# Gathers of a routed expert layer issued in pairs behind the matmul steps, and tile places reused oldest first

## The chip, the cores and the metric

The kernel runs on one core of a Trainium2 chip. The metric is the device time of one execution in microseconds (us). The engines are TensorE (PE, with its weight loads PEld), VectorE (DVE), ScalarE (ACT), GpSimd (POOL) and SyncE (SP, which issues most transfers). Each engine works its own instructions in the order of its own stream, and engines wait for each other by semaphores. An indirect gather is issued by POOL, which is busy while it does so; the rows land some microseconds later.

## The reference

Three layers follow each other on 2304 tokens of 512 numbers (4 x 8 heads x 576 x 64), all in 32-bit floats:

```python
kv = np.einsum('bhsd,bhse->bhde', k, v)                 # linear attention
out = np.einsum('bhsd,bhde->bhse', q, kv)
x = out / rms(out) * g_norm                             # 2304 x 512

top2 = np.argpartition(-noisy_logits, 2, axis=1)[:, :2] # 8 experts, 2 per token
for e in range(E):
    for k in range(2):
        mask = top2[:, k] == e
        h = np.maximum(x[mask] @ w1[e], 0.0)            # 512 -> 1024
        out[mask] += top2_w[mask, k, None] * (h @ w2[e])  # 1024 -> 512

gate = 1.0 / (1.0 + np.exp(-(x @ w_gate)))              # second layer, 512 -> 1536
return (gate * (x @ w_val)) @ w_out                     # 1536 -> 512
```

## The kernel before

**Numbers.** A 32-bit float goes through PE as two parts: ACT writes the high part (a tile whose name ends in h), DVE the rest (it ends in l), and a product takes three matmuls: high by high, high by low, low by high.

**Stages.** Up to about 130 us come the attention, the routing and expert e0. Experts e1 to e7 follow until about 549 us. Then comes the second layer: its first steps (up to about 575), its products (two chunks of the tokens, six pieces of the width, seven products per piece, which are added and subtracted to give a 2 x 2 block product), and from about 820 us the steps of the output.

**An expert.** Each expert takes up to 624 rows, in five blocks of 128. It has eight *h steps* (`h_step`, line 756 within `h_half`): 24 matmuls of 312 columns into `ph`, of which PSUM holds two. ACT then writes `hh` (line 761) and DVE `hl` (line 762); both must be done before PE's step after next, which writes the same `ph`. Five *y steps* follow (`y_step`, line 800): 24 matmuls of 512 columns into `py`, which ACT copies to `yo` and SP stores in `ybuf`.

**Gathers.** The rows of expert e+1 are gathered while e runs. `gather` (lines 687 to 697, through `rows_of`) issues four indirect gathers of quarter rows per block into an `xg` tile; there are four such tiles, so a gather waits until DVE has transposed the block that held its tile (line 743). `scale` (line 716) multiplies a block by its routing weights, on POOL. In the y phase `expert_in` takes a block in: DVE's transpose (743), ACT's `xh` (746), DVE's `xl` (747). In the loop over h steps, `gather(e + 1, i)` stands in steps 0 to 3 and `scale(e + 1, i - 1)` in steps 1 to 4, all in POOL's program order; the fifth block is gathered and scaled in the y phase. Nothing ties POOL to PE's steps: it runs as far ahead as its tiles allow. Beside this DVE sums and splits weights (lines 604 to 637, `raw`, `wg`, `wv`, `w_..`), paced by a planner (`pump`).

**The second layer's gathers.** `fetch` issues two gathers (`yg`, from `ybuf`) per tile of 128 tokens, which ACT scales and DVE adds. Tiles 0 to 3 are fetched within e7. Those of tiles 4 to 9, twelve gathers, stand one behind another in front of the layer's first steps. The first steps' matmuls are `pgv` (line 1121), the transposes `px` (1019); ACT copies the result to `q` (1129) and DVE multiplies it.

**Places.** The tiles of the second layer stand in places: 28 of the pool `wp` (`free`) and 11 of `g4` (`extra`). `place` takes the next of `free` while there is one, else one of `extra`; `drop` and `put_back` give places back. A tile that takes a place waits for whatever still reads the tile before it: a matmul, or a store of it. In the output steps `gr` is loaded from `qbuf`, and `gh_..h` (ACT, line 976) and `gh_..l` (DVE, line 977) are split from it for the matmuls `poa`, `pob`, `poc` (line 1332). The stores of `qt`, `qv` and `q` are lines 1197 to 1199.

**Order.** POOL and SP run in program order, DVE too after e0, PE and ACT in the second layer; in the experts a scheduler orders PE and ACT.

Of the kernel before, what the change touches and what calls it, by code (L numbers as in the profile page):

```python
# [9 lines left out]
FT = mybir.dt.float32  # L10
# [62 lines left out]
def tile_linear_attention_moe_glu(  # L73
# [16 lines left out]
    nc = tc.nc  # L90
# [11 lines left out]
    NB = CAP_BLOCKS  # L102
# [9 lines left out]
    QW = DM // 4 + KD  # L112
# [6 lines left out]
    WHOLE = CHUNKS[0][1]  # L119
# [4 lines left out]
    sml = ctx.enter_context(tc.tile_pool(name="sml", bufs=2))  # L124
# [14 lines left out]
    free = deque(range(28))  # L139

    def take(shape, dt, name):

        i = free.popleft()
        return i, wp.tile(shape, dt, tag="w", name=name)

    def wt(shape, dt, name):

        i, t = take(shape, dt, name)
        free.append(i)
        return t  # L150
# [7 lines left out]
    def et(shape, dt, name):  # L158
        return ep.tile(shape, dt, tag="e", name=name)
# [33 lines left out]
    first = ctx.enter_context(ExitStack())  # L193
# [16 lines left out]
    for i in range(B // 2):  # L210
        x = wt([128, 2, H, D], FT, f"vrem{i}")
# [35 lines left out]
    x, y = KD * 2 * E, KD * 2 * E + NT * E  # L247
# [327 lines left out]
    raws, wst, places, whole = deque(), {}, {}, set()  # L575
# [81 lines left out]
        return True  # L657

    def put_back(u):
        free.extend(places.pop(u))  # L660

    def pump(work_of_pe, own=0.0):

# [13 lines left out]

    XG, XA, XL, HH, HL = {}, {}, {}, {}, {}

    def whole_rows(e, blk):  # L680

        return e == 0 or e == 1 and blk < 2

    def gather(e, blk):
        if whole_rows(e, blk):
            x = et([128, XW], FT, "xg")
            a = e == 0 and blk < AB
            ix = lsa[:, blk:blk + 1] if a else lsb[:, blk * E + e:blk * E + e + 1]
            rows_of(x, xbuf[0:NA, :] if a else xbuf, ix)
        else:  # L690
            x = et([128, 4, QW], FT, "xg")
            for b in range(4):
                rows_of(x[:, b], xbuf.rearrange("n (a w) -> (n a) w", a=4), lsq[:, b, blk * E + e:blk * E + e + 1])
        XG[e, blk] = x

    def rows_of(x, src, ix):
        nc.gpsimd.indirect_dma_start(out=x, out_offset=None, in_=src,  # L697
                                     in_offset=bass.IndirectOffsetOnAxis(ap=ix, axis=0))
# [9 lines left out]
    def scale(e, blk, eng):  # L708
        x = XG[e, blk]
        if whole_rows(e, blk):  # L710
            i, t = take([128, DM], FT, f"xs{e}_{blk}")
            XG[e, blk] = scaled_rows(x, eng, t)
            places["xs", e, blk] = i,
        else:
            xv = x[:, :, 0:128].rearrange("p b (c j) -> p b c j", j=32)
            eng.tensor_mul(xv, xv, x[:, :, 128:, None].to_broadcast([128, 4, KD, 32]))  # L716
# [214 lines left out]
    def fetch(t):  # L931
        rows = (t + 1) * E * 128 if t < NB else (NB * E + OVB) * 128
        if t < NB - 1:
            YG[t] = [et([128, 4, 128], FT, f"yg{j}") for j in range(2)]
        else:
            YP[t], y = place([128, 2, 4, 128], FT, f"yg{t}")
            YG[t] = [y[:, 0], y[:, 1]]
        for j in range(2):
            yg = YG[t][j]
            rows_of(yg.rearrange("p b w -> p (b w)"), ybuf[0:rows, :], slot[:, t, j:j + 1])  # L940
# [52 lines left out]
    extra = deque()  # L993

    def place(shape, dt, name):
        if free:
            i, t = take(shape, dt, name)
            return (free, i), t
        return (extra, extra.popleft()), g4.tile(shape, dt, tag="g4", name=name)

    def drop(at):
        at[0].append(at[1])

    def x2_in(t, ps=None, js=(0, 1)):

# [30 lines left out]
    XS, XP, Q = {}, {}, {}  # L1036
# [481 lines left out]
    for e in range(E):  # L1518
        last = e == E - 1
        order = ExitStack()  # L1520
        if e == 0:
            order.enter_context(in_order("Activation"))
        for f in range(FC):
            if e:
                h_step(e, f)
            elif f % 2 == 0:
                h_first(f // 2, 1)
            if f % 2:
                put_back(("w1", e, f // 2))
            pump(*(3.53, HL_COST) if e else (4.15, 0.5))  # L1530
            if e or f > 1:
                fill()
            i = f
            if e == 0:

                for blk in range(NB - 1) if f == 0 else ():
                    gather(1, blk)
                if f == 1:
                    for blk in range(2):
                        scale(1, blk, nc.gpsimd)  # L1540
                    gather(1, NB - 1)
                if f > 1 and f % 2:
                    scale(1, f // 2 + 1, nc.gpsimd)
            elif not last:
                if i < NB - 1:
                    gather(e + 1, i)
                if 1 <= i < NB:
                    scale(e + 1, i - 1, nc.gpsimd)
        order.close()
        nxt = 0  # L1550
        for blk in range(AB if e == 0 else 0, NB) if not last else ():
            was = nxt
            while nxt < (NB if blk == NB - 1 else blk + 1):
                if nxt == 2 and e:
                    scale(e + 1, NB - 1, nc.gpsimd)
                with tc.high_priority(1):
                    expert_in(e + 1, nxt)
                if nxt == 0 and e:
                    gather(e + 1, NB - 1)
                nxt += 1  # L1560
            if (e, blk) == (2, 0):
                tc.mark_branch_hint_location("overflow", engines=ENGINES)
            with in_order("PE Activation") if (e, blk) == (1, 2) else nullcontext():
                y_step(e, blk, lambda f: ask_overflow() if (e, blk, f) == (1, 2, 3) else None)

            if (e, blk) != (2, NB - 1):
                pump(5.45, IN_COST * (nxt - was))
                if e:
                    fill()
        if not last:  # L1570
            for i in range(FP):
                put_back(("w2", e, i))
        if e == 2:
            assert len(filled) > OVB
            overflow()
            pump(5.45, IN_COST * (nxt - was))
# [23 lines left out]
    lw = ctx.enter_context(tc.tile_pool(name="lw", bufs=LOADS - AHEAD + 2))  # L1600
    g4 = ctx.enter_context(tc.tile_pool(name="g4", bufs=PLACES))
    extra.extend(range(PLACES))
    for t in range(NB - 1, WHOLE):
        fetch(t)


    firsts = [(p, j) for p in range(FP2) for j in range(2)]
    NF = len(firsts)
    steps = [(0, 0, 1)]
    for c in range(NCH):  # L1610
        for p in range(FP2):
            for n in PRODUCTS:
                x = (c, p, n) if n != 1 else (c + (p + 1) // FP2, (p + 1) % FP2, n)
                if x[0] < NCH:
                    steps.append(x)
    at = {x: k + NF for k, x in enumerate(steps)}
    events, now = {}, [0]

    def on(k, f, *x):
        events.setdefault(k, []).append((f, x))  # L1620
# [3 lines left out]
    def turn(t):  # L1624
# [3 lines left out]
            pair.extend((ps[:, 0], ps[:, 1]))  # L1628
        x2_in(t, pair.pop(0))

    for t in range(PLAIN, WHOLE):
        on(t - PLAIN, combine, t)
        on(t, turn, t)
# [64 lines left out]
    for k in range(Z + 3):  # L1698
# [14 lines left out]
        if NF <= k + AHEAD < z:  # L1713
            i = k + AHEAD
# [6 lines left out]
        elif k < z:  # L1721
            c, p, n = steps[k - NF]
            i, w = ready[k]
# [3 lines left out]
        elif k < Z:  # L1727
            c, n, u = osteps[k - z]
# [40 lines left out]
```

## Time and profile before

| | |
|---|---|
| runs of the kernel before | 971.55, 964.77, 969.79 us; median 969.79 |
| profiled execution | 966.0 us, of which 964.2 are its span |
| PE busy | 919.2 us, 95% |
| PEld busy | 792.9 us, 82% |
| DVE busy | 683.7 us, 71% |
| ACT busy | 440.3 us, 46% |
| POOL busy | 351.0 us, 36% |
| mean granted clock of PE | 0.989 |

The profile shows one execution. Busy time says how long an engine worked, not whether it was waited for. What one stage loses is read from PE's idle time in that stage and from what ended it: the views by window, by wait, and the timelines of single engines.

### The profile page before, as it was taken

To read this page: it belongs to the slowest core of one execution; us is meant where nothing else is said; L and a number is where in the kernel's file an instruction comes from. 1 tells how busy PE (TensorE), PEld (TensorE's weight loads), DVE (VectorE), ACT (ScalarE), POOL (GpSimd) and SP (SyncE) were. 2 spreads that over 40 slices of the span, in tenths; PEclk is the share of its full clock that TensorE was granted. 3 is DMA by queue.
4 is the path that set the end of the run, shared out by engine and by line. 5 is a ranking of instruction groups with operands and counts; after the bars stand their busy time and mean duration, and the time that the engine had idled before them with its cause. 6 is when DMAs were issued, how large, how long until landed. Compare 5 with 4: busy or idle time off the path is not lost.

```text
span 964.2 us, 14275 instructions
## 1 busy us (share of the span) xinstructions
PE 919.2 (95%) x5155; PEld 792.9 (82%) x5155; DVE 683.7 (71%) x1033; ACT 440.3 (46%) x659; POOL 351.0 (36%) x323
## 2 busy tenths in 40 slices
PE   7887998999999999999999989999999999989998
PEld 4876888889888887989899879888788888868886
DVE  2498679859777683978866448897977776866453
ACT  1673353424343432244433647655555555544451
POOL 2141586281263717156100353262355636300000
PEclk9997999999999999999999989999999999999999
DMA  9984678878776474466753466698477766876793
GB/s 265 283 274 162 191 240 285 275 246 282 249 219 218 129 254 134 142 233 194 253 162 103 130 188 185 221 287 294 151 253 262 261 236 248 313 254 204 213 281 99
DMA packets 134381, 213.93 MB, mean 222 GB/s; under 512 B 20384, under 2 KB 65952, under 8 KB 134304
## 3 DMA queue, kind: packets, MB, share of 16 engines
q1 hardware_dynamic: 122128, 190.05, 60.8%
q0 software_dynamic: 7664, 20.26, 7.4%
q10 hardware_dynamic: 4512, 2.66, 1.0%
q8 instruction: 41, 0.67, 0.3%
q14 instruction: 36, 0.29, 0.1%
HBM read 140.94 MB, written 71.97 MB: 221 GB/s over the span
## 4 chain that ended last, share of the span: by engine, by line
PE 56%; DVE 9%; DMA 3%; issue 2%; ACT 2%; another core or an unknown queue 1%; SPq 0%; DVEq 0%; ACTq 0%
PE pga L1153 12%; PE py L800 11%; PE poa L1332 7%; PE pgc L1153 6%; PE ph L756 6%; PE pgv L1121 4%; PE poc L1332 3%; PE pgb L1153 3%; PE pob L1332 2%; DVE hl L762 1%; DMA raw<-in_moe_w_val_dram 1%; DVE raw L611 1%; PE pout L1302 1%; DMA qbuf<-qv 1%
## 5 line engine op out<-in xcount | busy, mean ns | idle before, releaser
L697 POOL DMA_INDIRECT xg<-xbuf,lsq x132 | 140.5, 1064 | 156.3 <-DVE xT L743 106.8
L977 DVE TENSOR_TENSOR wt<-lw,wt 128x512 fp32r<-128x512 f32 x84 | 67.3, 807 | 37.4 <-ACT wt L976 34.7
L761 ACT ACTIVATE hh<-ph 128x624 fp32r<-128x624 f32 (+1 forms) x60 | 41.7, 696 | 107.6 <-PE ph L756 79.6
L762 DVE SCALAR_TENSOR_TENSOR hl<-ph,hh 128x624 fp32r<-128x624 f32 (+1 forms) x60 | 48.6, 810 | 54.0 <-ACT hh L761 44.5
L697 POOL DMA_INDIRECT yg<-ybuf,slot x36 | 39.1, 1085 | 110.6 <-DMA ybuf<-yo 45.4
L976 ACT ACTIVATE wt<-lw 128x512 fp32r<-128x512 f32 x84 | 50.1, 622 | 7.4 <-issue 4.2
L746 ACT ACTIVATE xh<-xT 128x512 fp32r<-128x512 f32 (+3 forms) x40 | 21.1, 544 | 68.9 <-DVE xT L743 60.2
L716 POOL TENSOR_TENSOR xg<-xg 128x512 f32<-128x512 f32 x33 | 37.5, 1139 | 38.7 <-DMA xg<-xbuf,lsq 38.4
L747 DVE TENSOR_TENSOR xl<-xT,xh 128x512 fp32r<-128x512 f32 (+3 forms) x40 | 24.9, 634 | 29.4 <-ACT xh L746 23.8
L805 ACT ACTIVATE yo<-py 128x512 f32<-128x512 f32 (+1 forms) x40 | 23.6, 589 | 45.5 <-PE py L800 34.8
L756 PE MATMUL ph<-xh,w_2h 128*128 128x312 f32 (+2 forms) x128 | 39.6, 310 | 4.9 <-DVE hl L762 4.1
L756 PE MATMUL ph<-xh,w_1h 128*128 128x312 f32 (+2 forms) x128 | 40.4, 315 | 3.8 <-DVE hl L762 3.5
L1167 ACT ACTIVATE q<-pga 128x1024 f32<-128x1024 f32 x24 | 24.7, 1027 | 41.3 <-PE pga L1153 36.2
L1121 PE MATMUL pgv<-x0h,w 128*128 128x256 f32 x192 | 39.6, 297 | 3.9 <-issue 3.2
L756 PE MATMUL ph<-xl,w_0h 128*128 128x312 f32 (+2 forms) x128 | 40.5, 316 | 2.4 <-DVE xl L747 2.2
L756 PE MATMUL ph<-xh,w_0h 128*128 128x312 f32 (+2 forms) x128 | 40.3, 316 | 2.1 <-issue 1.5
L756 PE MATMUL ph<-xh,w_0l 128*128 128x312 f32 (+2 forms) x128 | 40.1, 313 | 0.3 <-PEq L835 0.3
L756 PE MATMUL ph<-xh,w_3h 128*128 128x312 f32 (+2 forms) x128 | 39.4, 308 | 0.7 <-DVE hl L762 0.5
L1190 POOL TENSOR_TENSOR qt<-qv 128x512 f32<-128x512 f32 x12 | 18.0, 1502 | 59.7 <-PE pgc L1153 23.8
L756 PE MATMUL ph<-xl,w_1h 128*128 128x312 f32 (+2 forms) x128 | 39.7, 310 | 0.0
L756 PE MATMUL ph<-xh,w_1l 128*128 128x312 f32 (+2 forms) x128 | 39.6, 309 | 0.0
L756 PE MATMUL ph<-xh,w_3l 128*128 128x312 f32 (+2 forms) x128 | 39.3, 307 | 0.0
(557 smaller groups left out, 3085.0 us busy)
## 6 DMA issues: line engine op xcount, KB each, us to landing
raw<-in_moe_w_dram SPq DMA_DIRECT2D x60, 512.0 KB
lw<-wbuf SPq DMA_DIRECT2D x84, 256.0 KB
gr<-qbuf SPq DMA_DIRECT2D x42, 512.0 KB
ybuf<-yo SPq DMA_DIRECT2D x32, 256.0 KB
ybuf<-zero SPq DMA_DIRECT2D x29, 256.0 KB
raw<-in_moe_w_gate_dram SPq DMA_DIRECT2D x12, 512.0 KB
raw<-in_moe_w_val_dram SPq DMA_DIRECT2D x12, 512.0 KB
raw<-in_moe_w_out_dram SPq DMA_DIRECT2D x12, 512.0 KB
```

Of the source, the lines that this page charges most:

```text
L697: nc.gpsimd.indirect_dma_start(out=x, out_offset=None, in_=src, in_offset=bass.IndirectOffsetOnAxis(ap=ix, axis=0))
L716: eng.tensor_mul(xv, xv, x[:, :, 128:, None].to_broadcast([128, 4, KD, 32]))
L747: nc.vector.tensor_sub(XL[e, s][:, :, a:z], pt[:, :, o:o + z - a], XA[e, s][:, :, a:z].bitcast(FT))
L756: nc.tensor.matmul(ph, w[:, c, j], x[e, s][:, c, :], start=(n == 0), stop=(n == 3 * KD - 1))
L761: nc.scalar.activation(hh, ph, AF.Relu)
L762: nc.vector.scalar_tensor_tensor(hl, ph, 0.0, hh.bitcast(FT), op0=OP.max, op1=OP.subtract)
L800: nc.tensor.matmul(py[0:m], x[:, f % 2, t], w[:, f % 2, :], start=(n == 0), stop=(n == 3 * FC - 1))
L976: nc.scalar.activation(hi, src, AF.Copy)
L977: nc.vector.tensor_sub(lo, src, hi.bitcast(FT))
L1121: nc.tensor.matmul(pg[:, k // 2, 0:PC], w[:, a, d, s], X0[x][:, 2 * (k % 2) + d, :], start=(k % 2 == 0 and d + a + x == 0), stop=(k % 2 == ...
L1153: nc.tensor.matmul(ps[:, j, 0:HT[c]], w[:, a, k, s], x[:, k, :], start=(first and i == 0), stop=(i == 5), skip_group_check=not first)
L1332: nc.tensor.matmul(ps[:, j, 0:HT[c]], w, g[x][1][:, f, :], start=(first and u + f + i == 0), stop=(u == FP3 - 1 and f + i == 3), skip_grou ...
```

## The change

In e1 to e6 the sixteen gathers of blocks 0 to 3 become eight pairs, one in each h step. In front of every pair but the first, POOL copies one column (128x1) of the `hh` of the step before into a small tile `seen` (`behind`), so that POOL waits until ACT has written it. The scales of blocks 0, 1 and 2 stand in steps 3, 5 and 7, that of block 3 at the head of the y phase. In the second layer tiles 4 and 5 are fetched at once, and each of tiles 6 to 9 behind a copy of the `q` of the step before, one in each of the steps 1 to 4. And `place` now takes, of the two queues, the place that was given back earliest; `drop` numbers them, and `put_back` goes through it.

```diff
     def put_back(u):
-        free.extend(places.pop(u))
+        for i in places.pop(u):
+            drop((free, i))
...
+    def behind(x):
+
+        seen = sml.tile([128, 1], FT, name="seen")
+        nc.gpsimd.tensor_copy(seen, x)
+
...
-    def gather(e, blk):
+    def gather(e, blk, quarters=(0, 4)):
...
-            x = et([128, 4, QW], FT, "xg")
-            for b in range(4):
+            x = XG[e, blk] if quarters[0] else et([128, 4, QW], FT, "xg")
+            for b in range(*quarters):
...
     def place(shape, dt, name):
-        if free:
+
+        if free and not (extra and dropped.get((1, extra[0]), 0) < dropped.get((0, free[0]), 0)):
             i, t = take(shape, dt, name)
             return (free, i), t
         return (extra, extra.popleft()), g4.tile(shape, dt, tag="g4", name=name)
 
+    dropped = {}
+
     def drop(at):
         at[0].append(at[1])
+        dropped[int(at[0] is extra), at[1]] = max(dropped.values(), default=0) + 1
...
             elif not last:
-                if i < NB - 1:
-                    gather(e + 1, i)
-                if 1 <= i < NB:
-                    scale(e + 1, i - 1, nc.gpsimd)
+                if f:
+                    behind(HH[e, (f - 1) // 2].bitcast(FT)[:, (f - 1) % 2, 0:1])
+                gather(e + 1, i // 2, (2 * (i % 2), 2 * (i % 2) + 2))
+                if i % 2 and i > 1:
+                    scale(e + 1, i // 2 - 1, nc.gpsimd)
...
                 if nxt == 2 and e:
                     scale(e + 1, NB - 1, nc.gpsimd)
+                if nxt == 0 and e:
+                    scale(e + 1, NB - 2, nc.gpsimd)
...
-    for t in range(NB - 1, WHOLE):
+    for t in range(NB - 1, NB + 1):
         fetch(t)
...
+    def fetch_behind(t):
+
+        behind(Q["first", firsts[now[0] - 1][0]][1][:, firsts[now[0] - 1][1], 0:1])
+        fetch(t)
+
+    for t in range(NB + 1, WHOLE):
+        on(t - NB, fetch_behind, t)
```

The change moves POOL's instructions alone; the streams of PE, ACT, DVE and SP keep their order. First place: POOL in the h steps of expert e5, where the rows of e6 are gathered (`xg`), before. An "x4" stands for four gathers of one block, the TENSOR_TENSOR rows are the scales.

```order
L697 DMA xg_6146<-xbuf_93,lsq_242 128x132 x4
L697 DMA xg_6182<-xbuf_93,lsq_242 128x132 x4
L716 TENSOR_TENSOR xg_6146<-xg_6146 128x4x128
L697 DMA xg_6229<-xbuf_93,lsq_242 128x132 x4
L716 TENSOR_TENSOR xg_6182<-xg_6182 128x4x128
L697 DMA xg_6273<-xbuf_93,lsq_242 128x132 x4
L716 TENSOR_TENSOR xg_6229<-xg_6229 128x4x128
L716 TENSOR_TENSOR xg_6273<-xg_6273 128x4x128
```

The same place in the changed kernel, the h steps 0 to 5 (line 697 is line 703 there, 716 is 722):

```order
L703 DMA xg_6202<-xbuf_93,lsq_242 128x132 x2
L684 COPY seen_6236<-hh5_0_6163 128x1
L703 DMA xg_6202<-xbuf_93,lsq_242 128x132 x2
L684 COPY seen_6281<-hh5_0_6163 128x1
L703 DMA xg_6283<-xbuf_93,lsq_242 128x132 x2
L684 COPY seen_6324<-hh5_1_6240 128x1
L703 DMA xg_6283<-xbuf_93,lsq_242 128x132 x2
L722 TENSOR_TENSOR xg_6202<-xg_6202 128x4x128
L684 COPY seen_6363<-hh5_1_6240 128x1
L703 DMA xg_6365<-xbuf_93,lsq_242 128x132 x2
L684 COPY seen_6405<-hh5_2_6329 128x1
L703 DMA xg_6365<-xbuf_93,lsq_242 128x132 x2
```

Between two pairs there is now always a copy, and a scale only behind every second pair. Second place: POOL at the start of the second layer, before, where the tiles are numbered `yg4` to `yg9`.

```order
L697 DMA yg4_7679<-ybuf_94,slot_236 128x512 x2
L697 DMA yg5_7682<-ybuf_94,slot_236 128x512 x2
L697 DMA yg6_7685<-ybuf_94,slot_236 128x512 x2
L697 DMA yg7_7688<-ybuf_94,slot_236 128x512 x2
L697 DMA yg8_7691<-ybuf_94,slot_236 128x512 x2
L697 DMA yg9_7694<-ybuf_94,slot_236 128x512 x2
```

And in the changed kernel:

```order
L703 DMA yg4_7763<-ybuf_94,slot_236 128x512 x2
L703 DMA yg5_7766<-ybuf_94,slot_236 128x512 x2
L684 COPY seen_7804<-q0_0_7798 128x1
L703 DMA yg6_7806<-ybuf_94,slot_236 128x512 x2
L684 COPY seen_7855<-q0_0_7798 128x1
L703 DMA yg7_7857<-ybuf_94,slot_236 128x512 x2
L684 COPY seen_7901<-q0_1_7889 128x1
L703 DMA yg8_7903<-ybuf_94,slot_236 128x512 x2
L684 COPY seen_7953<-q0_1_7889 128x1
L703 DMA yg9_7955<-ybuf_94,slot_236 128x512 x2
```

Four copies stand between the gathers of the last four tiles. Third place: ACT at the output steps around 850 us, before, with what each instruction waits for (DMAHW2 is here the transfer that stores `qv`).

```order
L976 ACTIVATE gh0_t_2h_10293<-gr0_2_10216 128x512 [waits DMAHW4_49,DVE_49]
L976 ACTIVATE wos4h_10312<-sr4_10241 128x1024 [waits DMAHW5_49,DVE_49]
L976 ACTIVATE gh0_5_0h_10316<-gr0_5_0_10247 128x1024 [waits DMAHW6_49,DMAHW2_49,Pool_49]
L976 ACTIVATE wos5h_10339<-sr5_10266 128x1024 [waits DMAHW7_49,DVE_49]
L976 ACTIVATE gh0_5_1h_10343<-gr0_5_1_10272 128x1024 [waits DMAHW0_49,DVE_49]
L976 ACTIVATE gh0_5_2h_10361<-gr0_5_2_10297 128x1024 [waits DMAHW4_49]
```

And in the changed kernel:

```order
L982 ACTIVATE gh0_t_2h_10385<-gr0_2_10308 128x512 [waits DMAHW4_49,PE_49]
L982 ACTIVATE wos4h_10404<-sr4_10333 128x1024 [waits DMAHW5_49,DVE_49]
L982 ACTIVATE gh0_5_0h_10408<-gr0_5_0_10339 128x1024 [waits DMAHW6_49]
L982 ACTIVATE wos5h_10431<-sr5_10358 128x1024 [waits DMAHW7_49,PE_49]
L982 ACTIVATE gh0_5_1h_10435<-gr0_5_1_10364 128x1024 [waits DMAHW0_49,DVE_49,PE_49]
L982 ACTIVATE gh0_5_2h_10453<-gr0_5_2_10389 128x1024 [waits DMAHW4_49,PE_49,Pool_49]
```

`gh0_5_0h` waits for its own load (DMAHW6) in both, and for the store and POOL only before. On DVE the waits for the stores of `qt`, `qv` and `q` stand in the changed kernel at `wos5l`, `gh0_5_1l` and `gh0_5_2l`, and `wos4l` waits for a matmul 23 places earlier in PE's count.

## Rows read from the trace of the kernel before

**Rows 1.** The page: busy time, share of the span and instructions per engine.

```profile
PE 919.2 (95%) x5155; PEld 792.9 (82%) x5155; DVE 683.7 (71%) x1033; ACT 440.3 (46%) x659; POOL 351.0 (36%) x323
```

**Rows 2.** Windows over the h phases e1 to e7: length, each engine's busy time, clock, DMA.

```profile
147.20:179.10 31.90, 28.79 (x195) 27.75 (x194) 30.41 (x39) 12.09 (x17) 13.36 (x13) 1.00 0.84 274
206.00:233.60 27.60, 27.60 (x194) 27.59 (x193) 22.38 (x31) 10.25 (x14) 10.38 (x10) 1.00 0.67 227
260.80:291.60 30.80, 28.96 (x195) 27.77 (x194) 21.11 (x27) 12.57 (x17) 20.51 (x20) 1.00 0.76 239
319.00:348.20 29.20, 27.89 (x194) 27.61 (x193) 23.54 (x31) 10.83 (x15) 13.37 (x13) 1.00 0.51 159
375.30:409.20 33.90, 30.11 (x194) 28.99 (x193) 23.28 (x34) 7.50 (x11) 11.22 (x12) 0.95 0.39 117
436.40:465.80 29.40, 28.09 (x194) 27.58 (x193) 23.44 (x31) 12.26 (x17) 13.71 (x13) 1.00 0.63 205
492.90:520.50 27.60, 27.60 (x194) 27.60 (x193) 21.28 (x33) 12.25 (x17) 0.00 (x0) 1.00 0.42 134
```

**Rows 3.** PE's waits, the largest: us in total, times, longest.

```profile
PE ph L756 <- DVE hl L762: 8.1, 6, 1.9
```

**Rows 4.** Timeline of POOL in e4: start, us, instruction, and idle time before with its releaser.

```profile
326.15 1.07 POOL L716 TENSOR_TENSOR xg<-xg 128x512 f32<-128x512 f32 x1
...
332.13 1.07 POOL L716 TENSOR_TENSOR xg<-xg 128x512 f32<-128x512 f32 x1
334.78 1.54 POOL L716 TENSOR_TENSOR xg<-xg 128x512 f32<-128x512 f32 x1 [1.58 <-DMA xg<-xbuf,lsq]
```

**Rows 5.** Timeline of DVE in e4.

```profile
325.70 1.82 DVE L607 TENSOR_SCALAR wg<-wg 128x512 uint32<-128x512 uint32 x1
...
330.05 0.69 DVE L612 TENSOR_TENSOR wg<-wg,raw 128x512 f32<-128x512 f32 x1
...
335.44 1.42 DVE L612 TENSOR_TENSOR wg<-wg,raw 128x512 f32<-128x512 f32 x1
336.79 0.80 DVE L762 SCALAR_TENSOR_TENSOR hl<-ph,hh 128x624 fp32r<-128x624 f32 x1
```

**Rows 6.** Timeline of PE in e4, the one matmul with idle time before it.

```profile
337.64 0.41 PE L756 MATMUL ph<-xh,w_2h 128*128 128x312 f32 x1 [1.31 <-DVE hl L762]
```

**Rows 7.** Timeline of ACT in e3 and in e5.

```profile
282.87 0.69 ACT L761 ACTIVATE hh<-ph 128x624 fp32r<-128x624 f32 x1 [3.73 <-remote]
...
387.67 0.70 ACT L761 ACTIVATE hh<-ph 128x624 fp32r<-128x624 f32 x1 [3.72 <-remote]
```

**Rows 8.** Timeline of POOL at the second layer's start, first and last of twelve.

```profile
553.32 0.94 POOL L697 DMA_INDIRECT yg<-ybuf,slot  x1 [4.23 <-PE pgv L1121]
...
567.43 0.94 POOL L697 DMA_INDIRECT yg<-ybuf,slot  x1 [0.30 <-issue]
```

**Rows 9.** The chain of work there: start, us, work.

```profile
559.19 2.88 PE pgv L1121 x24
...
573.31 3.90 PE pgv L1121 x24
```

**Rows 10.** Timeline of ACT there.

```profile
560.46 0.39 ACT L1129 ACTIVATE q<-pgv 128x256 f32<-128x256 f32 x1 [1.51 <-PE px L1019]
...
570.48 0.38 ACT L1129 ACTIVATE q<-pgv 128x256 f32<-128x256 f32 x1 [6.47 <-remote]
```

**Rows 11.** Window over the steps behind, columns as in the windows above.

```profile
574.00:652.00 78.00, 78.00 (x428) 68.39 (x428) 66.28 (x91) 51.15 (x79) 30.91 (x24) 0.99 0.72 225
```

**Rows 12.** Timeline of PE at the output steps.

```profile
852.29 0.50 PE L1332 MATMUL poc<-gh_0h,wos0h 128*128 128x512 f32 x1 [1.99 <-ACT gh_0h L976]
...
853.55 0.50 PE L1332 MATMUL poc<-gh_0l,wos0h 128*128 128x512 f32 x1 [0.53 <-DVE gh_0l L977]
```

**Rows 13.** The chain of work there.

```profile
843.31 7.80 DMA qbuf<-qv
```

**Rows 14.** Groups of POOL's instructions: the smallest.

```profile
L1753 POOL MEMSET const-float32-0.0<- 128x1 f32 x1 | 0.1, 99 | 0.3 <-issue 0.3
```

## The prediction

> **What bounds the kernel now.** I read the shares of busy time first: PE is busy for 919.2 us, 95% of the span [rows 1], so about 45 us of PE's idle time is all that a change on POOL can give back. Where it lies I read from windows over the first phase (eight h steps) of each expert, e1 to e7 [rows 2]. Nobody gathers during e7, and it takes 27.60 us, all of it PE busy: eight steps of 3.45 us. e2, with gathers, takes 27.60 too. The others take 31.90, 30.80, 29.20, 33.90 and 29.40, which is 4.3, 3.2, 1.6, 6.3 and 1.8 too much, together **17.2 us**.
>
> What PE waits for there is DVE's hl of two steps ago: 8.1 us in 6 waits [rows 3]. Two things make hl late.
>
> First, POOL's scale. In e4, scales run at 326.15, 332.13 and 334.78 [rows 4], and the DVE instructions beside the first and the last are the long ones: L607 takes 1.82 us, and L612 at 335.44 takes 1.42 where the L612 at 330.05 takes 0.69 [rows 5]. The hl behind it starts at 336.79, and PE waits 1.31 us for it at 337.64 [rows 6]. The L612 at 330.05 stands in the same train of gathers, with no scale beside it, and isn't stretched. A step has room for one such delay: 3.45 less hh's 0.70 [rows 7] and hl's 0.80 [rows 5] leaves some 1.9 us, and a scale takes 1.07 to 1.54 us [rows 4] and can hold DVE no longer. Two that start 2.7 us apart, as those at 332.13 and 334.78, don't fit.
>
> Second, a late sign that PE has finished. ACT's hh at 282.87 (e3) and 387.67 (e5) start 3.7 us late with nothing recorded that they wait for but a remote signal [rows 7], while POOL issues gathers back to back. The same shows at the start of the second layer: twelve gathers stand back to back from 553.32 to 568.37, each 0.94 us with 0.30 between [rows 8]; PE's step before ends at 559.19 + 2.88 = 562.07, the step behind starts at 573.31, so one step with its short transposes has taken 11.2 us instead of 2.88, and the next takes 3.90 [rows 9]. ACT's q of the long step starts at 570.48 after 6.47 us of waiting for a remote signal [rows 10]. At most 8.4 + 1.0 = 9.4 us are lost there. Between 574 and 652 eight pairs of gathers come singly, and PE is busy for 78.00 of 78.00 us [rows 11]. So a pair alone is harmless, and a train of 12 to 16 is harmful at times: e2, e4 and e6 have such trains without that signature.
>
> A third place has nothing to do with gathers: at 852.29 PE waits 1.99 us for ACT's gh_0h, and right behind it 0.53 for DVE's gh_0l [rows 12]. gh_0h was held by the store of qv, 843.31 to 851.11 in the chain [rows 13]: the tile stood in a place given back only just before.
>
> **The change part by part.** *The copies.* 42 in the experts (seven in each of e1 to e6) and 4 in the second layer, 128x1. No such POOL copy is in the trace. The nearest row below is a MEMSET of 128x1 at 99 ns [rows 14]; the nearest above is the scale of 128x512, 1.07 us [rows 4]. I take 0.1 us. Behind a copy POOL's own queue waits, and only the gathers and the scale of that step: in a step 0.1 + 2 × 1.25 + 1.07 = 3.7 us with a scale, 2.6 without, 6.3 for two steps against PE's 6.9. POOL therefore keeps up. At the upper price it would be 8.2 for two steps, and the last pair would land some 5 us after the h phase; block 3 is wanted only in the fourth y step, so this costs PE nothing either. Nobody waits for `seen`.
>
> *The scales.* Three now stand in steps 3, 5 and 7, two steps (6.9 us) apart, block 3's at the head of the y phase. Each holds DVE for at most its own 1.07 to 1.54 us against the 1.9 of room. Waits of PE like that of e4 stand in e1, e4 and e6; at 1.31 each that is 3.9 us (part of the 8.1 of [rows 3]), and it should go.
>
> *The gathers.* They become pairs, one per step: eight pairs in the 27.6 us of every h phase. In before a large part of each train lay ahead of the phase. The pairs are closer (3.45 us) than those of 574 to 652 (about 10 us apart), so the harmless case isn't quite the new case. For e1 to e6 the bounds are: all like e2 and e7, −17.2; all like e3, 6 × 3.2 − 17.2 = +2.0; all like e5, 6 × 6.3 − 17.2 = +20.6. I take the mean of the three experts whose trains brought no late signal, e2, e4 and e6: (0 + 1.6 + 1.8)/3 = 1.13 each, 6.8 together: **−10.4 us**. It lies near the low end since the new density (two in 3.45 us) is below a train's (2.8).
>
> *The second layer.* Tiles 4 and 5 are gathered at once, 6 to 9 behind q of the first four steps. But the first gather can't start before 553.32 (the last rows of ybuf are landing), and ACT has done its q of the third step by 560.46 + 0.39 [rows 10], so that the q that the copies read is there by about 561, before POOL reaches the copies for tiles 6 to 8. So ten of the twelve gathers form the same train until 566, and the last pair alone is held. Bounds: 0 and −9.4. I take 2/12 of it, **−1.6 us**. If the late signal delays q, the copy holds POOL as well, which favours more.
>
> *The places.* With the earliest-returned place taken first, gh_0h waits for its load alone (third place of the order). The three stores' places go to wos5l, gh_1l and gh_2l, which DVE reaches after they landed. wos4l now waits for an earlier matmul of PE than before, so DVE can do it and gh_0l ahead of 850. I take both waits: **−2.5 us**, which is the bound on that side; the other is 0, if the stores' wait just moves on to the next tile.
>
> **The sum.** The profiled execution took 966.0 us: 966.0 − 10.4 − 1.6 − 2.5 = 951.5. The median of the runs shown is 969.8, 3.8 above it; the same ratio gives **955**.
>
> A rule of the Trainium skill speaks against half of this. SBUF — State Buffer, section "Who interferes with whom", says that PE and ACT never wait on anyone for SBUF, and that a DVE instruction with two SBUF inputs contends with a GpSimd instruction that reads SBUF. By its second half the stretched L612 beside a scale is what one expects, and the trace agrees (1.42 against 0.69); by its first half gathers can't be what stops PE, and rival A would be left. It speaks of SBUF's ports; whether a signal can come late it doesn't say.
>
> **The rivals.** *A: the late signals don't come from the gathers.* Then only the scales' waits (3.9) and the places (2.5) go: 966.0 − 6.4 = 959.6, as a median 963. It is the time by the Trainium skill's sentence on PE and ACT above. For it: e2, e4 and e6 had trains and no late signal. Against: every late signal fell in a train, none in e7.
>
> *B, the other side: the pairs bring the late signal to every expert.* Its place is hh of each step in e1 to e6: sixteen gathers now all lie inside the h phase, none ahead of it, and a late hh delays the next copy, so gathers bunch behind it. At e5's price in all six it is 966.0 + 20.6 − 2.5 = 984.1, as a median 988. At e3's price it is 966.0 + 2.0 − 2.5 = 965.5, median 969. It ends above the old time from (17.2 + 2.5)/6 = 3.3 us per expert on. For it: e3, the one expert with all sixteen inside its phase (20 POOL instructions in its window), had the signal. Against: e4 and e6 have as many POOL instructions in theirs as e1 and e5 (13, 13 against 13, 12) and lost only a scale's wait [rows 2].
>
> *C: all of it goes.* The trains are the whole cause and a copy that waits on q holds them off in the second layer as well: 966.0 − 17.2 − 9.4 − 2.5 = 936.9, median 941.
>
> *D: the binding doesn't bind.* Where hh is done before POOL comes to the copy, nothing changes. That holds for most of the second layer and is in the sum. In the experts each copy waits for an hh of the running phase, so it can't hold there; with it everywhere the time would be that of before less the places' 2.5: 963.5, median 967, and it has no more than 0.02 of A's chance.
>
> **How the numbers follow.** The main forecast 0.50, with its own range 947 to 960 (the experts keeping 0.5 to 2 us each); A 0.28, 959 to 968; B 0.13, 966 to 988; C 0.09, 938 to 946. Less than 1% can't be told from no change in this kernel, so faster means below 960 and slower above 979.5. Faster: nearly all of the main case, C, and an edge of A: 0.58. Slower: the upper half of B: 0.09. The same: 0.33. The range that leaves out the far half of B and of C is 942 to 972.
>
> **What would show it.** Right: the h phases of e1 to e6 at 28 to 29 us each; hl's waits gone from PE's list; DVE's long L607 and L612 still there, one to a scale, each alone; pairs of gathers 3.45 us apart; gh_0h done before 850 and no wait of poc for it. Wrong: hh that still starts 2 us and more after its matmuls, with pairs around it (B); a PE step of 11 us at 562 all the same (then the second layer's term is nothing); a DVE instruction waiting at 850 for the store of qv, qt or q. If the phases stay at 30 us and over with the scales spread, the scales were not the cause, and the experts' term fails.

## The result

The changed kernel takes 954.06 us (median of 6 runs, 953.23 to 958.1), the kernel before beside it 964.54 (6 runs, 963.55 to 971.55): ratio 0.9897, 95% interval 0.9866 to 0.9927. Its profiled execution took 954.98 us, with a span of 953.2 against 964.2. In the four further sets of runs, on four chips, the kernel before takes 950 to 952 us, and in the two of them that time the change it gains less than half as much: 0.9960 (0.9942 to 0.9978) and 0.9951 (0.9934 to 0.9968). That difference is part of what follows.

One correction ahead: the factor that `scale` applies is the attention's inverse root mean square, four per quarter row, and not a routing weight as said above. Nothing in the sum hangs on it.

The windows over the h phases e1 to e7 of the changed kernel, which answer to [rows 2], and behind them its y phases of e3, e4 and e5 (columns as there):

```profile
146.60:175.60 29.00, 28.40 (x195) 27.68 (x194) 26.89 (x39) 11.81 (x16) 19.69 (x20) 1.00 0.88 284
202.60:230.70 28.10, 27.76 (x194) 27.48 (x193) 22.03 (x31) 10.24 (x14) 19.17 (x21) 1.00 0.64 214
257.90:286.30 28.40, 28.10 (x195) 27.64 (x194) 21.40 (x28) 12.12 (x16) 20.71 (x22) 1.00 0.78 251
317.20:345.40 28.20, 27.86 (x195) 27.57 (x194) 21.72 (x29) 10.73 (x15) 20.45 (x20) 1.00 0.52 166
372.60:400.20 27.60, 27.60 (x194) 27.49 (x193) 21.11 (x33) 7.51 (x11) 17.78 (x21) 1.00 0.50 150
431.10:459.30 28.20, 27.86 (x195) 27.57 (x194) 21.57 (x28) 11.24 (x16) 20.11 (x20) 1.00 0.58 180
486.50:514.90 28.40, 28.06 (x194) 27.58 (x193) 22.55 (x35) 12.91 (x19) 0.00 (x0) 1.00 0.48 157
...
286.30:317.30 31.00, 28.96 (x121) 23.04 (x121) 21.24 (x31) 9.58 (x16) 12.19 (x12) 0.94 0.55 183
345.40:372.70 27.30, 27.30 (x122) 22.21 (x121) 19.71 (x26) 11.16 (x17) 12.48 (x13) 1.00 0.64 215
400.20:431.20 31.00, 29.11 (x122) 23.25 (x122) 25.18 (x35) 13.59 (x19) 11.64 (x12) 0.94 0.76 245
```

The h phases sum to 197.9 us, against 210.4 before: 12.5 are gained. But the y phases of e3 and e5 take 31.0 where e4's takes 27.3, which gives 7.4 back. PE's waits say for whom (us in total, times, longest):

```profile
PE py L806 <- DVE hl L768: 2.0, 1, 2.0
PE py L806 <- DVE w_3l L637: 1.9, 1, 1.9
...
PE ph L762 <- DVE hl L768: 1.3, 4, 0.3
```

The 8.1 us of [rows 3] have become 1.3. Two new waits stand at the first y step, and in this execution each costs nearly twice its length: behind the wait the granted clock falls for a while to the lower of its two levels, 1.2 GHz, and its mean over the next 3.6 and 4.0 us is 0.64 and 0.58.

```profile
293.40:297.00 3.60, 3.52 (x10) 2.79 (x11) 2.83 (x6) 1.11 (x2) 1.20 (x2) 0.64 0.47 146
406.40:410.40 4.00, 3.89 (x10) 3.11 (x11) 3.20 (x5) 2.36 (x4) 2.51 (x3) 0.58 0.78 283
```

The timelines of POOL, DVE and PE around the first of the two (e3), each line with its own engine:

```profile
290.36 1.07 POOL L722 TENSOR_TENSOR xg<-xg 128x512 f32<-128x512 f32 x1
292.10 1.52 POOL L722 TENSOR_TENSOR xg<-xg 128x512 f32<-128x512 f32 x1 [0.68 <-DMA xg<-xbuf,lsq]
...
289.94 2.04 DVE L611 SCALAR_TENSOR_TENSOR raw<-raw 128x512 f32<-128x512 uint32 x1
...
292.63 0.80 DVE L768 SCALAR_TENSOR_TENSOR hl<-ph,hh 128x624 fp32r<-128x624 f32 x1
...
293.48 0.50 PE L806 MATMUL py<-w_3h,hl 128*128 128x512 f32 x1 [2.04 <-DVE hl L768]
```

And of the second (e5):

```profile
403.10 1.06 POOL L722 TENSOR_TENSOR xg<-xg 128x512 f32<-128x512 f32 x1
...
402.90 1.82 DVE L1096 TENSOR_TENSOR ws5b<-wg,ws5a 128x512 f32<-128x512 f32 x1
...
406.51 0.50 PE L806 MATMUL py<-w_3l,hh 128*128 128x512 f32 x1 [1.89 <-DVE w_3l L637]
```

It is the signature of e4 in [rows 4 to 6], moved: a scale runs beside one of DVE's instructions, which takes 2.04 or 1.82 us where the same kind takes 0.69 with no scale beside it, and in DVE's order hl or w_3l stands behind it.

At the start of the second layer the chain of work and POOL's and ACT's timelines read:

```profile
553.61 2.88 PE pgv L1131 x24
...
566.60 3.31 PE pgv L1131 x24
...
563.95 0.18 POOL L684 COPY seen<-q 128x1 f32<-128x1 f32 x1 [2.77 <-DVE q L1142]
...
562.98 0.39 ACT L1139 ACTIVATE q<-pgv 128x256 f32<-128x256 f32 x1 [2.32 <-remote]
```

From 553.61 to 566.60 are 12.99 us, where [rows 9] have 14.12, and the step behind takes 3.31 instead of 3.90: 1.7 us less. The step itself, from 556.49 on, still takes 10.1 us. Ten gathers still form a train, and only the last pair was held, for 2.77 us. The way from the first `pgv` to the first `pga`, before and in the changed kernel:

```profile
549.40:596.10 46.70, 42.35 (x321) 40.80 (x322) 27.92 (x47) 26.63 (x52) 21.24 (x20) 0.93 0.61 182
...
543.80:588.70 44.90, 41.82 (x320) 41.06 (x321) 27.80 (x46) 26.98 (x52) 22.75 (x25) 0.92 0.65 194
```

At the output steps poc starts right behind pout, since ACT wrote gh_0h long ahead:

```profile
842.95 0.39 PE L1342 MATMUL poc<-gh_0h,wos0h 128*128 128x512 f32 x1
...
836.25 1.05 ACT L982 ACTIVATE gh_0h<-gr 128x1024 fp32r<-128x1024 f32 x1
```

No idle time stands before that matmul, nor before those that follow it: the waits of [rows 12] are gone, and so is one of 0.44 us behind them.

The copies, grouped (min, median and max in ns):

```profile
L684 POOL COPY seen<-hh x42: 182/312/1260, 153.0 to 459.9; 128x1 f32<-128x1 f32 x42
```

### The profile page after: what moved, and what is told of

The parts are those of the page before. It is cut to its first block, busy times and chain, and to the rows that moved or that the text cites. A ratio compares the mean times of both kernels' runs of the same rounds, so it can differ in the third digit from the quotient of the medians.

```text
span 953.2 us, 14355 instructions
## 1 busy us (share of the span) xinstructions
PE 919.9 (97%) x5155; PEld 795.6 (83%) x5155; DVE 690.0 (72%) x1033; ACT 439.1 (46%) x659; POOL 380.9 (40%) x369
## 4 chain that ended last, share of the span: by engine, by line
PE 57%; DVE 8%; DMA 3%; issue 3%; ACT 1%; DVEq 0%; SPq 0%; ACTq 0%
PE pga L1163 12%; PE py L806 11%; PE poa L1342 7%; PE ph L762 6%; PE pgc L1163 6%; PE pgv L1131 4%; PE poc L1342 3%; PE pgb L1163 3%; PE pout L1312 2%; PE pob L1342 2%; DVE hl L768 1%; DMA raw<-in_moe_w_dram 1%; DVE raw L611 1%; DMA raw<-in_moe_w_val_dram 1%; ACT hh L767 1%
## 5 line engine op out<-in xcount | busy, mean ns | idle before, releaser
L703 POOL DMA_INDIRECT xg<-xbuf,lsq x132 | 152.4, 1154 | 55.9 <-issue 32.5
L983 DVE TENSOR_TENSOR wt<-lw,wt 128x512 fp32r<-128x512 f32 x84 | 70.9, 850 | 33.2 <-ACT wt L982 27.3
L684 POOL COPY seen<-hh 128x1 f32<-128x1 f32 x42 | 19.4, 462 | 65.5 <-ACT hh L767 64.6
L1131 PE MATMUL pgv<-x0h,w 128*128 128x256 f32 x192 | 39.2, 297 | 3.3 <-issue 2.5
L762 PE MATMUL ph<-xh,w_2l 128*128 128x312 f32 (+2 forms) x128 | 39.2, 306 | 0.1
```

The costliest lines, as they stand in the source:

```text
L762: nc.tensor.matmul(ph, w[:, c, j], x[e, s][:, c, :], start=(n == 0), stop=(n == 3 * KD - 1))
L983: nc.vector.tensor_sub(lo, src, hi.bitcast(FT))
L1131: nc.tensor.matmul(pg[:, k // 2, 0:PC], w[:, a, d, s], X0[x][:, 2 * (k % 2) + d, :], start=(k % 2 == 0 and d + a + x == 0), stop=(k % 2 == ...
```

## The experiments

Each run stands beside runs of the kernel before on the same chip, in four sets. The medians of before are 951.88 (the parts alone), 950.25 (scales and trains), 951.10 (scales on DVE) and 950.36 us (before once more). In this section an e with a number is an expert, as above.

### The parts alone

**Experts alone**, the kernel before with

```diff
+                if f:
+                    behind(HH[e, (f - 1) // 2].bitcast(FT)[:, (f - 1) % 2, 0:1])
+                gather(e + 1, i // 2, (2 * (i % 2), 2 * (i % 2) + 2))
+                if i % 2 and i > 1:
+                    scale(e + 1, i // 2 - 1, nc.gpsimd)
...
+                if nxt == 0 and e:
+                    scale(e + 1, NB - 2, nc.gpsimd)
```

> The kernel before with the experts' part of the change alone (pairs behind copies of hh, scales in steps 3, 5, 7 and at the head of the y phase). If the terms that the two traces show add up (h phases -12.1 us, y phases of e3 and e5 +7.2 us): about 4.9 us faster than before, 959.6 against 964.5, with the PE gaps of 2.0 and 1.9 us in the y phases of e3 and e5 present. If the y phases' new waits come from another part of the change (places), they are absent and it is 12 us faster, 952.5.

Measured: 950.22 us, ratio 0.9977 (0.9959 to 0.9994), 1.7 us faster by the medians. The gaps in the y phases are there, so they come with this part, but the gain of the h phases is far smaller than in the first set. Neither number that was expected came, and the reason is that of the run of before below.

**The second layer alone**: `fetch_behind` for tiles 6 to 9 in the kernel before.

> The kernel before with the second layer's part alone (tiles 4 and 5 fetched at once, 6 to 9 behind copies of q). Theory (ten of the twelve gathers still form the train): 1.7 us faster, 962.8. Rival (the binding keeps the train off PE): up to 9 us faster, 955.5.

Measured: 951.40 us, ratio 1.0002 (0.9987 to 1.0017): nothing. With the old train (the run of the experts alone, whose second layer is that of before) as with the new one no PE step of this start is stretched by more than 0.7 us, and the way from the first `pgv` to the first `pga` takes 38.1 us with the old train and 38.8 with the new: here there is no loss to win back.

**The places alone**: `place`, `drop` and `put_back` of the change in the kernel before.

> The kernel before with the places alone (earliest given back goes first). Theory: PE's waits of 1.99, 0.53 and 0.44 us at 850 are gone and nothing else changes: 3.0 us faster, 961.5. Rival (the stores' wait moves on to another tile): 0 to 1 us faster.

Measured: 946.98 us, ratio 0.9941 (0.9923 to 0.9959). PE's waits at the output steps are gone, and no other stands in their place. The gain of 4.9 us is more than these waits; its interval goes down to 3.9. From the first `poa` to the end the trace shows 134.7 us, against 137.6 in the run of the second layer alone: 2.9 are read there, and what makes the rest is not known.

**Without the copies**, the changed kernel less

```diff
-                if f:
-                    behind(HH[e, (f - 1) // 2].bitcast(FT)[:, (f - 1) % 2, 0:1])
```

> The changed kernel without the 42 copies of hh in the experts; POOL's order of gathers and scales there is then that of before and runs as far ahead as the tiles allow. Theory (the copies make the experts' difference): the h phases of before return (+12 us) and the y phases' 7.2 us go: about 959, 4.9 us slower than the changed kernel. Rival (places and second layer change the experts' pace by themselves): 954, as the changed kernel.

Measured: 947.71 us, ratio 0.9955 (0.9938 to 0.9971): as much as the places give alone. The y phases' waits are gone, the h phases' are back.

### The kernel before without the late signals

> The kernel before, unchanged, for a trace of it from a set of runs like the last three. If the late signals belong to this kernel's trains of gathers, hh and q wait for remote signals as in its first profile (14.8 and 6.5 us), e5's h phase takes 33.8 us and the way from the first pgv to the first pga 46.6. If they belong to the first set of runs, these are 0, about 29.5 and 38.1, and the h phases e1 to e7 sum to about 203 us instead of 209.

Measured: 952.29 us, ratio 1.0008 (0.9987 to 1.0029). Its h phases e1, e3, e5 and e7, and the sum of all seven; then, from the run of the second layer alone, whose experts are those of before, e1 and the sum; last the way from the first `pgv` to the first `pga`:

```profile
151.80:179.80 28.00, 28.00 (x195) 27.67 (x195) 25.14 (x36) 11.81 (x16) 9.63 (x8) 1.00 0.83 263
...
262.00:291.80 29.80, 28.31 (x196) 27.70 (x195) 23.15 (x29) 12.89 (x17) 20.68 (x20) 1.00 0.76 250
...
375.00:405.60 30.60, 28.64 (x194) 27.57 (x193) 24.14 (x34) 7.45 (x11) 12.05 (x13) 1.00 0.44 131
...
489.00:516.50 27.50, 27.50 (x193) 27.40 (x193) 20.40 (x31) 12.26 (x17) 0.00 (x0) 1.00 0.38 116
sum 202.50, PE 196.08 PEld 193.04 DVE 163.19 ACT 77.66 POOL 81.39; mean PE 28.01 PEld 27.58 DVE 23.31 ACT 11.09 POOL 11.63
...
146.40:178.30 31.90, 28.70 (x194) 27.63 (x193) 30.41 (x40) 11.86 (x17) 13.42 (x13) 1.00 0.82 270
...
sum 203.10, PE 195.64 PEld 192.64 DVE 167.36 ACT 77.41 POOL 83.05; mean PE 27.95 PEld 27.52 DVE 23.91 ACT 11.06 POOL 11.86
...
545.80:585.00 39.20, 38.56 (x320) 38.13 (x321) 26.55 (x46) 26.52 (x52) 23.97 (x22) 1.00 0.73 222
```

ACT's group of hh says what its idle time ended with, in the first profile of before, in the profile of the change, and here:

```profile
L761 ACT ACTIVATE hh<-ph 128x624 fp32r<-128x624 f32 (+1 forms) x60 | 41.7, 696 | 107.6 <-PE ph L756 79.6 <-remote 14.8 <-issue 7.9
```

```profile
L767 ACT ACTIVATE hh<-ph 128x624 fp32r<-128x624 f32 (+1 forms) x60 | 41.6, 697 | 97.7 <-PE ph L762 74.1 <-issue 19.5 <-remote 2.7
```

```profile
L761 ACT ACTIVATE hh<-ph 128x624 fp32r<-128x624 f32 (+1 forms) x60 | 41.7, 697 | 97.2 <-PE ph L756 97.2
```

The same kernel with the same trains of gathers has 14.8 us of waits for a remote signal in the first set and none here; none of the other eleven traces has any either. So the late signals belong to the first set of runs, not to the trains as such. That they are PE's can be read from the first trace: each of the five waits of hh ended with a semaphore that PE alone raises, 2.0 to 4.7 us after the end that the profile gives for the matmul before it.

What they cost is not the whole of 210.4 less 202.5. Of these 7.9 us, 3.9 stand in e1, which has no such wait in either trace: here e1 starts 4.6 us later, behind a y phase of e0 that is 6.1 us longer, and in the run of the second layer alone it takes 31.9 as in the first set, without a late signal. Over e2 to e7 the first trace has 178.5 us, this one 174.5 and the run of the second layer alone 171.2. So 4.0 to 7.3 us of the 17.2 of [rows 2] were the late signals', nearly all of it in e3 and e5. More is lost at the start of the second layer, where q waits 6.47 us for such a signal [rows 10]: it takes 46.7 us in the first set and 39.2 here. The 7.5 us there and the 4.0 make up most of the 12.9 by which the spans differ (964.2 and 951.3).

### Scales or gathers

**Before without the scales** of the blocks of e2 to e7 (that factor is not applied to them).

```diff
-                if 1 <= i < NB:
-                    scale(e + 1, i - 1, nc.gpsimd)
...
-                if nxt == 2 and e:
-                    scale(e + 1, NB - 1, nc.gpsimd)
```

> The kernel before with the scales of the gathered blocks of e2 to e7 left out (the routing weight is not applied to these blocks; everything else runs). Theory (without late signals the h phases lose time only through POOL's scales beside DVE): the h phases of e3, e4, e5 and e6 fall from 29.0, 29.0, 29.5 and 28.6 to 27.5 us, about 6 to 9 us faster than before in all. Rival (the gathers cost it): the h phases stay as they are.

Measured: 941.83 us, ratio 0.9903 (0.9868 to 0.9938), 8.4 us faster. Its h phases of e2, e4 and e6, and the sum over seven:

```profile
203.30:230.70 27.40, 27.40 (x194) 27.40 (x193) 20.80 (x31) 10.26 (x14) 3.78 (x4) 1.00 0.69 227
...
313.30:340.70 27.40, 27.40 (x194) 27.40 (x193) 20.74 (x32) 10.95 (x15) 5.85 (x5) 1.00 0.52 161
...
422.80:450.20 27.40, 27.40 (x194) 27.40 (x193) 20.10 (x30) 11.81 (x16) 3.77 (x4) 1.00 0.57 187
...
sum 194.20, PE 192.98 PEld 192.24 DVE 149.49 ACT 77.66 POOL 41.02; mean PE 27.57 PEld 27.46 DVE 21.36 ACT 11.09 POOL 5.86
```

The gathers are all there, in the same trains, and PE has no gap in these phases: 194.2 against 202.5. Without late signals the loss of the h phases is the scales', save what stays in e1 and e3 (29.0 and 28.2 in the same view). Over e2 to e7, which leaves out the shifted e1, the h phases take 165.2 us against 174.5, or against 171.2 in the run of the second layer alone. DVE's instructions agree: of L608, L611 and L612 the first trace of before has 14 in e1 to e7 with a scale beside them, which take up to 2.10 us, and 94 without one, none over 0.75; here none of the 108 takes over 0.75.

**The change, and the scales of blocks 2 to 4 later.**

```diff
-                if i % 2 and i > 1:
+                if i in (3, 5):
                     scale(e + 1, i // 2 - 1, nc.gpsimd)
...
-                if nxt == 2 and e:
-                    scale(e + 1, NB - 1, nc.gpsimd)
-                if nxt == 0 and e:
-                    scale(e + 1, NB - 2, nc.gpsimd)
+                if 0 < nxt < 4 and e:
+                    scale(e + 1, nxt + 1, nc.gpsimd)
```

> The changed kernel once more, beside the others. If no late signals of PE show in this set of runs either (no hh and no q that waits for a remote signal), the parts measured alone give: places -4.9, experts -1.7, second layer 0 against before, so some 6 to 7 us faster than before (ratio 0.993). If the late signals show, 10 us (0.9897), as in the first comparison.

> The changed kernel with the scales of blocks 2 and 3 moved out of step 7 and the head of the y phase: they stand behind block 4's gathers, which wait for DVE's first transpose of the y phase; block 4's scale one y step later. Theory (the scale beside DVE's chain holds hl and w_3l back at the change of phase): PE's gaps of 1.5 to 2.0 us in the y phases of e3 and e5 go and with them the lowered clock behind, 4 to 7 us faster than the changed kernel. Rival (DVE's own chain of weight work is what is late there): the gaps stay, same time.

Measured: the change 947.39 us, 2.9 us faster than before and not the 6 to 7 that its parts alone would add up to; why they don't add up is not known. With the scales later 943.12, ratio 0.9917 (0.9889 to 0.9946): 4.3 us faster than the change. The y phase of e5 falls from 29.4 to 28.3 us and that of e3 from 30.8 to 28.7, with a gap left:

```profile
293.22 0.50 PE L806 MATMUL py<-w_3h,hl 128*128 128x512 f32 x1 [1.30 <-DVE hl L768]
...
286.93 0.66 ACT L604 ACTIVATE wv<-raw 128x512 f32<-128x512 f32 x1 [3.60 <-DMA raw<-in_moe_w_val_dram]
287.49 1.25 ACT L767 ACTIVATE hh<-ph 128x624 fp32r<-128x624 f32 x2
```

No scale runs beside DVE there any more. So of the two waits in e3 and e5 (1.9 each in that set) 0.6 and 1.2 us were the scale's; what stays in e3 is DVE's own chain, six instructions of weight work ahead of hl, which started late behind a late hh. And hh is late since ACT first waits 3.60 us for a load of weights, so that the hh of the last two steps follow it back to back. The rival was right for the larger part of e3's wait.

The change of this set also shows that the clock need not fall. Its e5 has the same wait for w_3l, 1.88 us, but the phase takes 29.5 and not 31.0 us:

```profile
400.80:430.30 29.50, 27.62 (x123) 22.20 (x122) 25.15 (x35) 13.58 (x19) 12.60 (x12) 1.00 0.80 253
407.10:411.10 4.00, 3.92 (x17) 3.27 (x18) 3.30 (x5) 2.83 (x4) 2.35 (x2) 1.00 0.77 283
```

**The same with trains** instead of pairs: two trains of eight gathers, in steps 0 and 3. Copies stand in steps 3 and 7 alone, with the scales of blocks 0 and 1 behind them.

```diff
-                if f:
+                if f in (3, 7):
                     behind(HH[e, (f - 1) // 2].bitcast(FT)[:, (f - 1) % 2, 0:1])
-                gather(e + 1, i // 2, (2 * (i % 2), 2 * (i % 2) + 2))
...
+                    scale(e + 1, f // 4, nc.gpsimd)
+                if f in (0, 3):
+                    gather(e + 1, 2 * (f // 3))
+                    gather(e + 1, 2 * (f // 3) + 1)
```

> The changed kernel with the scales spaced as in the run that moves them later, but the gathers in two trains of eight (behind steps 0 and 3) instead of a pair a step. Theory (without late signals pairs and trains cost the same, only the scales' places matter): the time of the run with the scales moved later, within 2 us. Rival (trains delay PE by themselves): h phases of e1 to e6 over 29 us, 6 us and more slower than that run.

Measured: 944.01 us, ratio 0.9934 (0.9909 to 0.9958), 0.9 us from the run before it: no difference that can be told.

**The scales on DVE**, which beats both kernels: the changed kernel with

```diff
+        if e > 1:
+            scale(e, blk, nc.vector)
         x = XG.pop((e, blk))
```

in `expert_in` and no scale on POOL for these blocks; then the same without the copies.

> The changed kernel, beside the two below. Without late signals of PE: 0.996 of before, as in the set before. With them: 0.990.

> The changed kernel with the scales of e2 to e7's blocks taken off POOL: DVE does each right ahead of its transpose of the block, in the y phase. DVE has 0.69 us more per block there, five per expert, and no instruction beside a POOL scale any more. Theory (what is left of the experts' loss is DVE beside POOL's scale): h phases 27.5 us but e1 and e3, no gap over 0.7 us in the y phases, 6 to 9 us faster than the changed kernel, near the run of before without scales. Rival (DVE's 3.5 us more per y phase hold w or xl back): gaps before py or ph for DVE, no faster than the changed kernel.

> The same without the 42 copies: POOL runs its gathers in trains, as far ahead as the tiles allow. Without late signals: the same time as the run with pairs, within 2 us. With late signals in this set (hh that waits for a remote signal): 5 us and more slower than the run with pairs, if the trains bring them on; the same, if they come whatever POOL does.

Measured: the change 946.29 us, with the scales on DVE 941.62, ratio 0.9896 (0.9861 to 0.9930), and without the copies 942.40, ratio 0.9906 (0.9873 to 0.9939). The 4.7 us from the change are less than the 6 to 9 expected. DVE takes 0.69 us for a scale:

```profile
L722 DVE TENSOR_TENSOR xg<-xg 128x512 f32<-128x512 f32 x30 | 20.5, 685 | 0.4 <-DMA xg<-xbuf,lsq 0.4
```

The scale costs DVE 0.69 us there. One on POOL stretched the DVE instructions shown by 0.7 (L612 in [rows 5]), 1.1 (L1096) and 1.35 us (L611). No gap of PE over 0.7 us is left in the y phases. The copies are worth 0.8 us, within the scatter.

## Why the prediction was right, and where not

**The time.** 955 was forecast and 954.1 measured; on the profiled execution 951.5 was forecast and 955.0 came. The sum is right to 3.5 us because two terms were off to opposite sides, and the median to 1 us by luck on top of it. It was scaled up from 969.8, the median of three runs; the six have 964.54. So the gain that was forecast is 14.8 us, a ratio of 0.985, and the measured one 10.5, a ratio of 0.9897 whose interval begins at 0.9866: the size of the gain was missed, and a base that was too high hid it. Of the 11.0 us between the two spans the four terms below give 9.8; the rest is in none of them.

**The h phases**: −10.4 forecast, −12.5 measured. In the first set both causes named were present, and neither shows in these phases of the changed kernel. But their shares were mis-sized. The scales were priced at 3.9 us from three waits like e4's; leaving them out (the run of before without scales) gave 8.4 us. The late signals made up 4.0 to 7.3 of the 17.2. Whether the pairs took them away can't be told from one execution of each kernel.

**The y phases**: 0 forecast, +7.4 measured. This step failed. The working held each scale against the room of a step in the h phase, 1.9 us, and gave its place at the head of the y phase no price. It asked when block 3 is wanted, and not which DVE instruction runs beside the scale and who waits behind that one. Two of its steps failed by its own terms: a scale was to hold DVE no longer than it takes, but beside one of 1.07 us L611 took 1.35 more; and two that start 2.7 us apart were said not to fit, but in e3 the last two start at 290.36 and 292.10, since the copy in step 7 waited for the late hh. At the change of phase the first y step takes hl of the last h step and the last weights at once, and DVE has no room there. The run without the copies shows that these waits go, but for 0.5 us in e3, when POOL runs ahead as before; the runs with the scales later and on DVE show that they shrink or go with the scale's place. About half of the 7.4 is the lowered clock, which the same wait in e5 did not bring in two later sets (1.88 and 1.82 us, phases of 29.5 and 29.4).

**The second layer**: −1.6 forecast, −1.7 measured in the first set, and 0 in the run of that part alone, where there was nothing to lose. That ten of the twelve gathers would still form the train held to the gather. The number is luck: a share of 2 in 12 was a guess, a step of 10.1 us stands where the prediction named one of 11 as a sign that the term is nothing, and one execution of each kernel can't tell 1.7 us of it from chance.

**The places**: −2.5 forecast; the two waits and the 0.44 behind them are gone in the trace, −3.0, and alone they gave 4.9 (3.9 to 7.3 by the interval). The waits that DVE now has for the stores cost PE nothing.

**The copies**: 0.1 us each forecast, 0.31 in the median and up to 1.26 measured. They delay nobody but POOL, as said: ACT's hh also waits for the copy of the hh that held its place before, but in the trace none was held by one, and the nearest had ended 0.7 us before.

**Rival A** was half right: a train of gathers doesn't by itself make PE's signals late, since none of the twelve runs behind the first set has them, and four of these have the experts' trains of before. What makes them, and why the first set alone had them, stays open. In the long step of the second layer PE's own matmuls stand apart too, with nine gaps (4.3 us in all) that the profile puts down to nothing that it records. In that set the kernel with pairs had one such wait in hh, of 2.74 us, where the one with trains had 14.8; it stands at 124.48 in e0, beside the first gathers for e1, which the change leaves in a train, and the ten-gather train still had one of 2.32. That fits trains as a condition, but it is one execution each, and no later set could test it. Where the signals are absent, a pair a step is worth nothing over a train (944.0 against 943.1, 942.4 against 941.6), and the change (0.9960 and 0.9951 of before) gains no more than the places alone (0.9941). **Rival B** is out: it needed 3.3 us more per expert; of the h phases e2's rose by 0.5, e7's, which has no gathers, by 0.8, and the others fell, and none has a late signal.

The prediction's rule from the Trainium skill (SBUF — State Buffer, "Who interferes with whom": a DVE instruction with two SBUF inputs contends with a GpSimd instruction that reads SBUF) bore more of the time than the sum gave it. By the rows it holds for L611 and L1096, at 1.1 to 1.35 us a scale. It does not cover L607 of [rows 5], which has one input and took 1.82 us beside a scale and 0.43 without; by the measurement the contention reaches further than that sentence.

## What to carry to other kernels

An instruction moved on an idle engine is not free when it stretches a busy engine's instruction, as POOL's scale did DVE's: ask what runs beside it at its new place and who stands behind that, above all at a change of phase, where several results are due at once. If a short operation on the idle engine stretches the busy one by more than the operation would cost there, move it there. And before a loss is put down to a pattern of the program, look whether every place with the same pattern has it: the trains of experts e2, e4 and e6 had no late signal. A run of the old kernel in a second set would have shown it at once.

## What the runs showed of the hardware that was not expected

A POOL copy of 128x1 takes 182 to 1260 ns, 312 in the median: 2 to 13 times the smallest MEMSET (99 ns, [rows 14]), and three times in the median.

In both new waits DVE's instruction had begun before the scale (289.94 against 290.36, 402.90 against 403.10), and by the profile it was DVE's that was stretched, by 1.35 and 1.14 us, more than the 1.07 and 1.06 that the scale took.

A wait of PE of 1.9 to 2.0 us in the y phase lengthened that phase by 3.7 in the first set, with the clock at its lower level behind it. But the clock does not fall behind every such wait: it did not behind 1.88 and 1.82 us for the same w_3l in two later sets, nor behind the 1.99 of [rows 12] (1.00 over the next 3.6 us), nor behind the 1.31 in e4 [rows 6], where the phase's clock is 1.00 [rows 2].

And one kernel takes 964 us in one set of runs and 950 to 952 in four others, with the same program and the same granted clock (0.989 in both profiled executions): the difference that the traces show is mostly waits of ACT for signals of PE that come late.
